# One tiled stage for R, A scores, C v and denominators; G in two stages; normalising among the inverse steps; two batches' u in one tile

## The chip, the cores and the metric

The kernel runs on one core of one Trainium2 chip. The metric is device time in microseconds (us), the median of several executions. A run has a state: fast, or slow when it lies over 1.5% above the fastest run of the same kernel. Engines in the profile: PE is TensorE's matmuls, PEld its weight loads, DVE is VectorE, ACT is ScalarE, POOL is GpSimd, SP is SyncE. L345 is line 345 of the kernel that the profile belongs to, so one statement has different lines in different kernels.

## The reference

Nyström attention with 32 landmarks over 8 batches of 8 heads, then a gated product without a nonlinearity:

```python
q_lm = q.reshape(B, H, m, S // m, D).mean(axis=3)     # B, H, S, D = 8, 8, 576, 64; m = 32
k_lm = k.reshape(B, H, m, S // m, D).mean(axis=3)
A  = softmax(q @ k_lm.T);  Bm = softmax(q_lm @ k_lm.T);  C = softmax(q_lm @ k.T)   # each scaled by 1/8
Z = Bm.T / (norm1(Bm) * norminf(Bm) + 1e-6)
for _ in range(6):
    Z = 2 * Z - Z @ Bm @ Z
x = (A @ Z @ C @ v)              # heads side by side: 4608 x 512
out = ((x @ w1) * (x @ w2)) @ w3 @ w_out
```

The kernel multiplies w3 and w_out together first (the "weight fold") and forms G = Z C v [w1, w2] for each batch. R in the title is the product of Bm with its transpose, from which the inverse steps for Z start. The "up products" are A times G; their elementwise product u is `ab` in the code. The output products are u times (w3 w_out), in chunks of 128 rows.

## The kernel before

The schedule is by hand: the attention of the next batch is a Python generator that yields between stages. The main loop runs one stage after an up product or an output product, so that VectorE's work on a stage hides behind TensorE's work on this batch.

The parts, with cuts marked:

```python
        scores_a(0)                       # A scores, first head group
        yield
        scores_a(1)
        # ... def cv(qd, es, psV): C v of 4 heads and its row sums, then DVE reads psV
        cv(0, es0, small())
        yield
        cv(1, es1, bank())
        yield
        # ...
        def denominators():               # row sums of exp(A scores), into a "big" buffer
            ps = big()
            # ... 8 matmuls into ps[:, 0, 0:QS]
            return ps

        def inverted(i):                  # reciprocals: from PSUM, into PSUM
            sl = slice(QS // 3 * i, QS // 3 * (i + 1))
            nc.vector.reciprocal(out=psS[:, 1, sl], in_=psS[:, 0, sl])

        def mixed():
            rr = psS[:, 1, 0:QS]          # rr is in PSUM
            rhi = pat.tile([128, QS], FP16, name="rhi", bufs=1)
            nc.vector.tensor_copy(out=rhi, in_=rr)
            rmix = pat.tile([128, QS], FP16, name="rmix")
            nc.vector.scalar_tensor_tensor(out=rmix, in0=rhi, scalar=lomask[:, 0:1], in1=rr,
                                           op0=ALU.mult, op1=ALU.add)
            return rmix
        # ... normalise(qd, rmix): 4 matmuls spread rmix over the rows, DVE multiplies
        for it in range(6):               # inverse steps
            # ... 16 small matmuls, then tz_ and sz_ by DVE
            if it == 1:
                psS = denominators()
            elif it in (2, 3, 4):
                inverted(it - 2)
            elif it == 5:
                rmix = mixed()
            yield
        # ... Z, normalise(0), yield, normalise(1), then G in four stages
```

The kernel's PSUM pool has three "big" buffers of 128 x 2 x 512 fp32, one "small" and one "acc" of 128 x 512 each; a "bank" in this text is 512 such columns. The first output chunk uses "acc", the next "big", and so on in turn. Meanwhile POOL adds up the landmarks of a later batch:

```python
    eng.tensor_tensor(out=tr, in0=x[:, :, 0, :], in1=x[:, :, 1, :], op=ALU.add)   # eng = POOL, 128 x 768
    eng.tensor_tensor(out=tr, in0=tr, in1=x[:, :, 2, :], op=ALU.add)              # 128 x 768
```

The softmax here doesn't subtract the row's maximum and nothing guards it: scores larger than these inputs give would overflow.

## Time and profile before

| | before |
|---|---|
| median of 3 runs | 300.87 us (299.02 to 301.57) |
| span of the profiled run | 299.0 us |
| TensorE busy | 276.5 us, 92% |
| mean granted TensorE clock | 0.987 |

The head of the profile's page. The rows below "2" cut the span into 40 slices and give tenths of busy time; PEclk is the granted TensorE clock in tenths.

```profile
PE 276.5 (92%) x4026; PEld 151.7 (51%) x4026; DVE 177.9 (59%) x454; ACT 124.3 (42%) x199; POOL 135.6 (45%) x176
...
PE   6867999999879989999999998999999999999993
...
PEclk9998999999979999999999999999999999999999
```

TensorE is the bound: after the first four slices and up to the last it is at 70% or more in every slice, and at 90% or more in most. So I count a microsecond in which it waits as about a microsecond of time.

What TensorE waited for, in us, times, and the longest (the view of waits, kernel before):

```profile
PE small L183 <- DVE parts L174: 2.7, 2, 2.4
PE big L100 <- DMA qkn<-in_k_dram: 2.7, 1, 2.7
...
PE big L426 <- ACT a_sb L430: 1.9, 9, 0.2
...
PE big L369 <- issue: 1.0, 1, 1.0
```

Most of these belong to start-up and to the passage from the weight fold to the main loop (the 2.4 us). "issue" is a wait for which the trace shows no semaphore.

### The profile page before, as it was taken

The page shows a single profiled execution, that of the slowest core. Times are in us where ns is not written, and L with a number is a line of the kernel's source. Part 1 is how long each engine was busy: PE and PEld are TensorE (multiplying, and loading weights), DVE is VectorE, ACT ScalarE, POOL GpSimd, SP SyncE. Part 2 cuts the span into 40 slices and gives each one's busy share as a digit, 9 for nine tenths or more (in the row PEclk, how much of TensorE's full clock was granted, in tenths as well). Part 3 has the DMA queues.
Part 4 walks back from the last instruction along what each step waited for, and adds up shares of the span by engine and source line. Part 5 has one row for each costly group of instructions (what it writes and reads, how often), then busy time and mean ns, then how long its engine had stood idle before and what let it go on. Part 6 is the DMA issues. An engine that isn't in the chain of part 4 may idle for free.

```text
span 299.0 us, 9452 instructions
## 1 busy us (share of the span) xinstructions
PE 276.5 (92%) x4026; PEld 151.7 (51%) x4026; DVE 177.9 (59%) x454; ACT 124.3 (42%) x199; POOL 135.6 (45%) x176
## 2 busy tenths in 40 slices
PE   6867999999879989999999998999999999999993
PEld 3434555444446447445744663366447535743741
DVE  8922743465476576755765765476666655765720
ACT  2113442233344266236625741474167236525531
POOL 1608132270009958950994499039918940600000
PEclk9998999999979999999999999999999999999999
DMA  6999999939920948975996999379949632013124
GB/s 242 279 268 255 239 232 230 164 38 196 203 54 8 214 110 172 224 165 104 186 219 150 147 201 202 101 140 203 228 111 154 154 107 70 4 30 79 36 58 118
DMA packets 61385, 45.56 MB, mean 152 GB/s; under 512 B 34976, under 2 KB 53408, under 8 KB 61344
## 3 DMA queue, kind: packets, MB, share of 16 engines
q1 hardware_dynamic: 46896, 31.86, 47.1%
q0 software_dynamic: 13632, 11.54, 24.8%
q10 hardware_dynamic: 816, 1.57, 1.4%
q8 instruction: 31, 0.51, 0.7%
q14 instruction: 10, 0.08, 0.1%
HBM read 38.80 MB, written 9.44 MB: 161 GB/s over the span
## 4 chain that ended last, share of the span: by engine, by line
PE 73%; DMA 9%; DVE 9%; ACT 6%; issue 2%; POOL 0%; ACTq 0%; DVEq 0%
PE big L426 16%; PE acc L446 13%; PE big L446 10%; PE acc L490 9%; DMA qkn<-in_q_dram 6%; PE big L412 6%; DVE ab L432 4%; PE big L369 4%; ACT a_sb L430 3%; DMA wof<-in_moe_w_out_dram 2%; PE small L305 2%; PE acc L305 2%; PE big L477 2%; PE big L353 1%; PE big L224 1%
## 5 line engine op out<-in xcount | busy, mean ns | idle before, releaser
L426 PE MATMUL big<-ahat,gt 128*128 128x288 f16 x512 | 75.1, 288 | 3.1 <-ACT a_sb L430 1.9
L432 DVE TENSOR_TENSOR ab<-a_sb,big 128x576 f16<-128x576 f16 x64 | 47.9, 750 | 19.5 <-PE big L426 7.7
L430 ACT CAST a_sb<-big 128x576 f16<-128x576 f32 x64 | 41.0, 640 | 41.6 <-PE big L426 36.1
L426 PEld LDWEIGHTS <-gt 128*128 128x128 f16 x512 | 47.6, 98 | 20.7 <-issue 5.8
L235 POOL TENSOR_TENSOR t<-ect 96x384 f32<-96x384 f32 x16 | 16.0, 997 | 87.0 <-ACT ect L228 86.5
L490 PE MATMUL acc<-wsp,w3t 128*128 128x512 f16 x168 | 42.1, 384 | 1.6 <-DVE wsp L471 0.9
L446 PE MATMUL acc<-w,ab 128*128 128x512 f16 (+1 forms) x192 | 41.0, 382 | 0.1
L446 PEld LDWEIGHTS <-ab 128*128 128x128 f16 (+1 forms) x320 | 23.9, 100 | 32.4 <-issue 9.3
L446 PE MATMUL big<-w,ab 128*128 128x512 f16 x128 | 32.8, 381 | 0.0
L166 POOL TENSOR_TENSOR tr<-qkT 128x768 f32<-128x768 f16 x14 | 23.0, 1643 | 20.7 <-DMA qkT<-qkn 11.0
L418 DVE TENSOR_SCALAR gt<-big 128x1024 f16<-128x1024 f32 x16 | 19.5, 1224 | 17.7 <-PE big L412 17.7
L490 PEld LDWEIGHTS <-w3t 128*128 128x128 f16 x192 | 18.1, 100 | 20.1 <-issue 4.1
L452 ACT ACTIVATE o_sb<-acc 128x512 f32<-128x512 f32 x20 | 11.9, 597 | 37.4 <-PE acc L446 35.5
L167 POOL TENSOR_TENSOR tr<-tr,qkT 128x768 f32<-128x768 f32 x14 | 23.0, 1641 | 1.1
L416 ACT ACTIVATE gt<-big 128x1024 f16<-128x1024 f32 x16 | 16.4, 1024 | 8.6 <-PE big L412 8.6
L412 PE MATMUL big<-wup,zt 64*32 64x512 f16 x512 | 19.0, 380 | 0.8 <-DVE ahat L356 0.8
L483 DVE SCALAR_TENSOR_TENSOR w3t<-big,w3t 128x512 f16<-128x512 f32 x16 | 11.0, 689 | 14.1 <-ACT w3t L482 14.1
L452 ACT ACTIVATE o_sb<-big 128x512 f32<-128x512 f32 x16 | 9.6, 598 | 22.4 <-PE big L446 22.4
L482 ACT ACTIVATE w3t<-big 128x512 f16<-128x512 f32 x16 | 9.5, 597 | 19.9 <-PE big L477 19.5
L228 ACT ACTIVATE ect<-big 96x768 f32<-96x768 f32 x16 | 12.9, 807 | 2.9 <-PE big L224 2.4
L356 DVE TENSOR_TENSOR ahat<-eat,big 128x576 f16<-128x576 f16 x16 | 11.9, 749 | 1.8 <-PE big L353 1.8
L172 POOL TENSOR_TENSOR o<-o,tr 128x256 f32<-128x256 f32 x14 | 11.2, 799 | 1.1
(311 smaller groups left out, 358.9 us busy)
## 6 DMA issues: line engine op xcount, KB each, us to landing
vt<-in_v_dram SPq DMA_DIRECT2D x8, 1152.0 KB, 8.5
qkn<-in_k_dram POOLq DMA_DIRECT2D x8, 576.0 KB, 10.8
qkn<-in_q_dram POOLq DMA_DIRECT2D x8, 576.0 KB, 13.4
out_dram<-o_sb SPq DMA_DIRECT2D x24, 192.0 KB, 2.3
w3f<-in_moe_w_dram SPq DMA_DIRECT2D x6, 512.0 KB, 7.5
out_dram<-o_sb SPq DMA_DIRECT2D x24, 128.0 KB, 2.4
wup<-in_moe_w_dram POOLq DMA_DIRECT2D x4, 512.0 KB, 24.9
wof<-in_moe_w_out_dram ACTq DMA_DIRECT2D x3, 512.0 KB, 7.3
```

The source lines that it names most:

```text
L166: eng.tensor_tensor(out=tr, in0=x[:, :, 0, :], in1=x[:, :, 1, :], op=ALU.add)
L167: eng.tensor_tensor(out=tr, in0=tr, in1=x[:, :, 2, :], op=ALU.add)
L235: nc.gpsimd.tensor_tensor(out=t3[0:NP], in0=e[:, :, 0:3, :], in1=e[:, :, 3:6, :], op=ALU.add)
L412: nc.tensor.matmul(psG[32 * h:32 * h + 32, qd, :], zt[rs, i, h, :], wup[rs, h, w, fs], start=(i == 0), stop=(i == 1), tile_position=(64 * ...
L416: nc.scalar.activation(out=g[:, :, w, fs], in_=psG, func=AXF.Copy, scale=1.0 / ZS)
L418: nc.vector.tensor_scalar(out=g[:, :, w, fs], in0=psG, scalar1=1.0 / ZS, scalar2=None, op0=ALU.mult)
L426: nc.tensor.matmul(p[:, c, 0:HS], st["g"][:, qd, w, 128 * j:128 * j + 128], st["ahat"][qd][:, c, :], start=(qd == 0), stop=(qd == 1))
L430: nc.scalar.copy(out=st["a_sb"], in_=p[:, :, 0:HS])
L432: nc.vector.tensor_tensor(out=st["ab"][:, j, :].rearrange("p (c s) -> p c s", c=2), in0=st["a_sb"], in1=p[:, :, 0:HS], op=ALU.mult)
L446: nc.tensor.matmul(pso[o:o + sz, :], ab[:, j, s0:s0 + sz], w34[:, j, :], start=(j == 0), stop=(j == 7), tile_position=(0, o))
L452: nc.scalar.activation(out=o_sb, in_=pso[:, :], func=AXF.Copy, scale=1.0 / (X64 * X64))
L490: nc.tensor.matmul(psW[j][:, :], turned[j, c // 4][:, a, c % 4, :], wsp[:, b, c, :], start=(c == 0 and a + b == 0), stop=(c == 7 and a == 1))
```

## The change

The intent, as I read it: a change of TensorE's tiling mode costs some 94 ns in the trace of before (a 288-column matmul is followed after 216 instead of 122 ns), so put the small tiled products of a batch into one stage, make G in two stages rather than four, and let u of two batches share one tile, so that no output chunk needs two half-height matmuls. The denominators share a PSUM tile with the C v products. The reciprocals `rr` go to SBUF. And normalising moves up among the inverse steps. The diff, cut to its core:

```diff
-        psR = bank()
+        psX = bank()                        # one tile: R, second C v group, denominators
...
         scores_a(0)
-        yield
         scores_a(1)
...
-        cv(0, es0, small())
-        yield
-        cv(1, es1, bank())
-        yield
+        cv(0, es0, psX if bank is small else small())
+        cv(1, es1, psX[:, 192:] if bank is small else psX)
+        for qd in range(2):
+            for c in range(4):
+                nc.tensor.matmul(psX[32 * c:32 * c + 32, 320:320 + QS],   # denominators
+                                 ...)
+        rr = pat.tile([128, QS], FP32, name="rr", bufs=1)                 # SBUF
         yield
...
-            nc.vector.reciprocal(out=psS[:, 1, sl], in_=psS[:, 0, sl])
+            nc.vector.reciprocal(out=rr[:, sl], in_=psX[:, 320 + sl.start:320 + sl.stop])
...
+        for i in range(3):
+            inverted(i)
+            if i < 2:
+                yield
         for it in range(6):
...
             if it == 1:
-                psS = denominators()
-            elif it in (2, 3, 4):
-                inverted(it - 2)
-            elif it == 5:
                 rmix = mixed()
+            elif it in (2, 3):
+                normalise(it - 2)
             yield
...
-        normalise(0, rmix)
         yield
-        normalise(1, rmix)
...                                          # G: yield after two blocks, not after each
-            steps(at, (0, 0, 0, 1, 1, 1, 2, 2)[j] if b == 0 else 1)
+            steps(at, (0, 0, 0, 1, 1, 1, 1, 0)[j] if b == 0 else (1, 1, 1, 0, 1, 0, 1, 1)[j])
             up(st, j, 1)
+        steps(at, 1)
```

The warm-up matmuls became 20 of 256 columns instead of 10 of 512, to free SBUF for the shared tile.

More of the change, by code (lines that the diff above doesn't have):

```diff
@@ L287, in attention @@
                 sl = slice(32 * h, 32 * h + 32)
-                nc.tensor.matmul(psR[sl, 32 * qd:32 * qd + 32], bt[sl, qd, :], bt[sl, qd, :],
+                nc.tensor.matmul(psX[sl, 128 + 32 * qd:160 + 32 * qd], bt[sl, qd, :], bt[sl, qd, :],
                                  start=True, stop=True, tile_position=(32 * h, 32 * h))
@@ L292, in attention @@
         for qd in range(2):
-            nc.vector.tensor_scalar(out=sz_[:, qd, 0:32], in0=psR[:, 32 * qd:32 * qd + 32],
+            psR = psX[:, 128 + 32 * qd:160 + 32 * qd]
+            nc.vector.tensor_scalar(out=sz_[:, qd, 0:32], in0=psR,
                                     scalar1=nrn[:, qd:qd + 1], scalar2=None, op0=ALU.mult)
             nc.vector.scalar_tensor_tensor(
-                out=tz_[:, qd, :], in0=psR[:, 32 * qd:32 * qd + 32], scalar=nrn[:, qd:qd + 1],
+                out=tz_[:, qd, :], in0=psR, scalar=nrn[:, qd:qd + 1],
                 in1=eye2[:, qd, :], op0=ALU.mult, op1=ALU.add)
         scores_a(0)
-        yield
         scores_a(1)
@@ L315, in cv @@
                                     scalar1=rcr[:, 0:1], scalar2=None, op0=ALU.mult)
-        cv(0, es0, small())
-        yield
-        cv(1, es1, bank())
-        yield
-        ahat = []
-        psS = None
-        def denominators():
-            ps = big()
-            for qd in range(2):
-                for c in range(4):
-                    nc.tensor.matmul(ps[32 * c:32 * c + 32, 0, 0:QS],
-                                     onesq[:, qd].rearrange("p a b h -> p (a b h)"),
-                                     eat[qd][:, QS * c:QS * (c + 1)],
-                                     start=(qd == 0), stop=(qd == 1), tile_position=(0, 32 * c))
-            return ps
+        cv(0, es0, psX if bank is small else small())
[3 more added lines that the diff above has]
+                nc.tensor.matmul(psX[32 * c:32 * c + 32, 320:320 + QS],
+                                 onesq[:, qd].rearrange("p a b h -> p (a b h)"),
+                                 eat[qd][:, QS * c:QS * (c + 1)],
+                                 start=(qd == 0), stop=(qd == 1), tile_position=(0, 32 * c))
+        rr = pat.tile([128, QS], FP32, name="rr", bufs=1)
+        yield
         def inverted(i):
             sl = slice(QS // 3 * i, QS // 3 * (i + 1))
-            nc.vector.reciprocal(out=psS[:, 1, sl], in_=psS[:, 0, sl])
+            nc.vector.reciprocal(out=rr[:, sl], in_=psX[:, 320 + sl.start:320 + sl.stop])
         def mixed():
-            rr = psS[:, 1, 0:QS]
             rhi = pat.tile([128, QS], FP16, name="rhi", bufs=1)
@@ L348, in mixed, with normalise @@
             return rmix
-        def normalise(qd, rmix):
+        ahat = st["ahat"] = []
+        def normalise(qd):
             psD = big()
@@ L396, in attention @@
                                        op0=ALU.mult, op1=ALU.subtract)
-        normalise(0, rmix)
         yield
-        normalise(1, rmix)
-        st["ahat"] = ahat
         g = st["g"] = pat.tile([128, 2, 2, DF], FP16, name="gt")
@@ L419, in attention @@
                                             scalar2=None, op0=ALU.mult)
-                yield
+            yield
     def up(st, j, w):
@@ L432, in up, with down @@
             nc.vector.tensor_tensor(
-                out=st["ab"][:, j, :].rearrange("p (c s) -> p c s", c=2),
+                out=st["ab"][:, j, st["t0"]:st["t0"] + S].rearrange("p (c s) -> p c s", c=2),
                 in0=st["a_sb"], in1=p[:, :, 0:HS], op=ALU.mult)
     rows = out.rearrange("(b p g) f -> b g p f", b=B, g=6)
-    def down(srcs, half, hold, bank):
+    def down(ab, b0, t0, half, hold, bank):
         if half == 0:
@@ L443, in down @@
         for j in range(4 * half, 4 * half + 4):
-            o = 0
-            for _, ab, s0, sz in srcs:
-                nc.tensor.matmul(pso[o:o + sz, :], ab[:, j, s0:s0 + sz], w34[:, j, :],
-                                 start=(j == 0), stop=(j == 7),
-                                 tile_position=(0, o))
-                o += sz
+            nc.tensor.matmul(pso[:, :], ab[:, j, t0:t0 + 128], w34[:, j, :],
+                             start=(j == 0), stop=(j == 7))
         if half == 1:
@@ L454, in down @@
             o = 0
-            for b, _, s0, sz in srcs:
-                while sz:
-                    gi, p0 = divmod(s0, NP)
-                    n = min(sz, NP - p0)
-                    nc.sync.dma_start(out=rows[b, 2 * (gi % 3) + gi // 3, p0:p0 + n, :],
-                                      in_=o_sb[o:o + n, :])
-                    o, s0, sz = o + n, s0 + n, sz - n
+            while o < 128:
+                gi, p0 = divmod((t0 + o) % S, NP)
+                n = min(128 - o, NP - p0)
+                nc.sync.dma_start(out=rows[b0 + (t0 + o) // S, 2 * (gi % 3) + gi // 3, p0:p0 + n, :],
+                                  in_=o_sb[o:o + n, :])
+                o += n
     def fold(pf, wof, w3f, wsp):
@@ L544 @@
         load_w3(1, 1)
-        warm = pf.tile([128, 512], FP16, name="warm", bufs=1)
+        warm = pf.tile([128, 256], FP16, name="warm", bufs=1)
         nc.vector.memset(warm, 0.0)
         psw = big()
-        for _ in range(10):
-            nc.tensor.matmul(psw[:, 0, :], warm[:, 0:128], warm, start=True, stop=True)
+        for _ in range(20):
+            nc.tensor.matmul(psw[:, 0, 0:256], warm[:, 0:128], warm, start=True, stop=True)
         nc.gpsimd.tensor_copy(out=gate, in_=wof[1][:, 0, 0:1])
@@ L589 @@
         load_qk(sts[2], 2)
-    pab = ctx.enter_context(tc.tile_pool(name="pab", bufs=3))
+    pab = ctx.enter_context(tc.tile_pool(name="pab", bufs=2))
     at = attention(sts[1], acc)
@@ L595 @@
         st = sts[b]
-        ab = st["ab"] = pab.tile([128, 8, S], FP16, name="ab")
+        if b % 2 == 0:
+            ab = pab.tile([128, 8, 2 * S], FP16, name="ab")
+        st["ab"], st["t0"] = ab, S * (b % 2)
         if b + 2 < B:
@@ L599 @@
             load_v(sts[b + 2], b + 2)
-        if b % 2 == 0:
-            chunks = [[(b, ab, 128 * t, 128)] for t in range(4)]
-        else:
-            chunks = [[(b - 1, sts[b - 1]["ab"], 512, 64), (b, ab, 0, 64)]]
-            chunks += [[(b, ab, 64 + 128 * t, 128)] for t in range(4)]
+        chunks = range(0, 512, 128) if b % 2 == 0 else range(512, 2 * S, 128)
         for j in range(8):
@@ L620 @@
             bank = (lambda: big()[:, 0, :]) if n // 2 % 2 else acc
-            down(chunks[n // 2], n % 2, hold, bank)
-            steps(at, 2 if n == 6 and nd == 8 else 1)
+            down(ab, b - b % 2, chunks[n // 2], n % 2, hold, bank)
+            steps(at, 2 if b == 0 and n == 0 else 1)
         steps(at, 30)
```

## The prediction

> **What bounds the kernel now.** TensorE. The page has it busy 92% of the span (DVE 59%, ACT 42%, POOL 45%); table of windows: 25.8 of 26.5 us in the batches with four output chunks, about 28 of 29 in those with five. The waits of TensorE sum to only some 17 us, most of it start-up. The first 33 us wait for loads, which the change leaves alone. So what counts is TensorE's time per batch, with its bubbles.
>
> **What it removes.** [...]the last 288-column matmul of an up product is followed after 122 ns by one of its own mode, after 216 ns by a tiled one; for 512 columns 216 and 309 ns. About 94 ns per entry; leaving costs about as much (L310 to L426 103 ns against 12 within the mode). Per batch the instruction order shows 8 to 10 fewer changes of mode. From starts in the timeline, R, A, C v, denominators and the first inverse step took 3.7 us plus six entries, in one stage they need 2.5 plus one, and one 0.42 us inverse step moves to the output phase: 0.8 us saved per batch. G in two stages saves 0.2 to 0.4 us.
>
> **What it adds: waits.** The semaphores of the built program show three new ones on TensorE, in every batch:
> 1. Denominators wait for DVE to have read the second C v group from the same PSUM tile. From the last ones matmul: 0.30 us to the reciprocal, ending with the scaled copy at 0.78. Bubble: about 0.85 us.
> 2. The first output chunk needs the "acc" bank, held until the third reciprocal slice is read. DVE alternates 0.75 us products and 0.46 us reciprocals behind the last up products: ready about 1.5 us after the last up product; the inverse step fills 0.33. Bubble: about 1.1 us.
> 3. Up products now run seven groups back to back. With three big buffers that costs 1.08 us a pair (batch 7, 277.9 to 285.5) against 0.98: 0.3 us with the waits of the A scores. rmix costs 0.2 us before the first normalisation.
>
> Sum: 0.8 to 1.2 us saved against 2.4 lost: odd batches about 1.1 us longer, even ones 1.5. The first batch of the loop has its stage and all three reciprocals directly before the first chunk, and Z, zt and both G stages behind the last: about 2 us longer. Attention inside the weight fold: about even. The whole sits on the critical path. 300.9 + 3 x 1.1 + 3 x 1.5 + 2 is 310.5; I shade it to 309, as the change looks tuned.
>
> **Predicted:** 309.0 us, 301.5 to 314.5 (8 in 10). Faster by over 2%: 0.08; within 2%: 0.24; slower by over 2%: 0.68.
>
> **What would show it.** Right: fewer mode changes; idle before denominators (releaser: DVE scaled copy of C v) of 0.7 to 1.0 us per batch; idle before the first output matmul (releaser: DVE reciprocal) of 0.8 to 1.4 us; time from the second C scores to the first output chunk longer by about a microsecond although its TensorE work is shorter; reciprocals, 0.46 us each, among the last up products on DVE. TensorE's busy share falls.
> Wrong: both bubbles under 0.3 us, and a batch of four chunks taking under 26.5 us.
>
> **What would make it wrong.** DVE running earlier than I chain it (the reciprocals ending before the last up product, say); [...]a larger saving per mode change for fp32 passes than 94 ns; cheaper G stages.

The cost of a mode change is the 94 ns of the trace, and the sum stands at 310.5, shaded to 309. The "fp32 passes" are records of the trace of before: it has 48 records for the 24 fp32 matmuls of one C v group (L305).

## More of the kernel before

The two DVE instructions that make rmix, with minimum, median and maximum duration in ns (the view of one tile, kernel before):

```profile
L344 DVE CAST rhi<-big x8: 297/297/298, 62.0 to 270.0; 128x144 f16<-128x144 f32 x8
L346 DVE SCALAR_TENSOR_TENSOR rmix<-rhi,lomask,big x8: 363/365/365, 62.3 to 270.3; 128x144 f16<-128x144 f16 x8
```

They take the same time in all eight batches. `big` in their names says that their source is a PSUM buffer.

## The result, and the profile after

A ratio here is the mean time of one kernel's fast runs over the mean of the other's fast runs of the same rounds, so it is not quite the ratio of the medians quoted.

| | before | after |
|---|---|---|
| median | 300.5 us (299.02 to 301.57, 4 runs) | 331.87 us (329.29 to 337.81, 4 runs, one of them slow) |
| ratio of fast runs | | 1.1019, 95% interval 1.0897 to 1.1141 |
| span of the profiled run | 299.0 us | 332.1 us |
| TensorE busy | 276.5 us, 92% | 283.0 us, 85% |
| mean granted TensorE clock | 0.987 | 0.954 |

The change made the kernel 10% slower. The direction was foretold. The size was not: 331.87 lies far outside 301.5 to 314.5.

The same head of the page, kernel after:

```profile
PE 283.0 (85%) x4004; PEld 157.0 (47%) x4004; DVE 186.7 (56%) x454; ACT 123.2 (37%) x199; POOL 134.9 (41%) x176
...
PE   6969979998776993899969986999699789979994
...
PEclk9989999999989896999987999899989999999999
```

TensorE now has slices at 60 and 70% all along the run (one at 30%), and the clock has several at 60 to 80%. Idle time grew from 22.5 to 49.1 us (span less busy time), which is 26.6 of the 33.1 us by which the span is longer. The other 6.5 us are longer busy time.

TensorE's waits, kernel after:

```profile
PE big L345 <- DVE rmix L336: 10.5, 5, 2.7
PE acc L435 <- DVE rr L330: 7.5, 7, 1.2
PE acc L321 <- issue: 4.4, 1, 4.4
...
PE acc L321 <- DVE sz__2286 L314: 0.7, 1, 0.7
```

The second line and the last (one such line of 0.6 or 0.7 us for each of the eight batches) are the two foretold bubbles. The first and the third were not foretold, and they are larger.

The two instructions that make rmix, kernel after:

```profile
L334 DVE CAST rhi<-rr x8: 224/988/1672, 55.1 to 299.4; 128x144 f16<-128x144 f32 x8
L336 DVE SCALAR_TENSOR_TENSOR rmix<-rhi,lomask,rr x8: 369/1243/1751, 55.3 to 299.7; 128x144 f16<-128x144 f16 x8
```

These are the same two operations on the same 128x144 elements, with `rr` in SBUF instead of PSUM. Their fastest case is as fast as before or faster (224 against 297 ns), and their slowest is about five times as slow. Something holds them up in some batches only. The timeline of one batch shows what (start, duration, engine, idle time before in brackets; DVE, POOL and PE lines, kernel after):

```profile
168.93 1.04 PE L435 MATMUL acc<-w,ab 128*128 128x512 f16 x4
168.93 1.64 POOL L166 TENSOR_TENSOR tr<-qkT 128x768 f32<-128x768 f16 x1
...
169.51 1.15 DVE L334 CAST rhi<-rr 128x144 f16<-128x144 f32 x1
...
170.65 1.63 POOL L167 TENSOR_TENSOR tr<-tr,qkT 128x768 f32<-128x768 f32 x1
170.70 1.75 DVE L336 SCALAR_TENSOR_TENSOR rmix<-rhi,lomask,rr 128x144 f16<-128x144 f16 x1
...
172.50 0.66 PE L345 MATMUL big<-rmix,selc 128*128 128x144 f16 x4 [2.22 <-DVE rmix L336]
...
172.96 1.91 PE L435 MATMUL big<-w,ab 128*128 128x512 f16 x4
```

The POOL addition at 168.93 ends at 170.57, and rhi ends at 170.66. The next addition ends at 172.28, and rmix ends at 172.45. Each of these two DVE instructions lasts until the POOL instruction that was already running is over, plus about 0.1 to 0.2 us. The last two lines show the sequel: TensorE stood for 2.22 us, and then the same four matmuls of 512 columns that took 1.04 us at 168.93 took 1.91. From start to start they are 427 ns apart, against 216 before the wait: half the clock, and the clock record has 0.5 from 171.93 to 178.76. The batch after the last POOL addition, in the same run, has the same two instructions without that neighbour:

```profile
299.41 0.23 DVE L334 CAST rhi<-rr 128x144 f16<-128x144 f32 x1
299.68 0.37 DVE L336 SCALAR_TENSOR_TENSOR rmix<-rhi,lomask,rr 128x144 f16<-128x144 f16 x1
```

In the kernel before, POOL's same addition also ran next to rhi (213.27 to 214.91), and rhi kept its duration, with its source in PSUM:

```profile
213.27 1.64 POOL L167 TENSOR_TENSOR tr<-tr,qkT 128x768 f32<-128x768 f32 x1
...
214.66 0.30 DVE L344 CAST rhi<-big 128x144 f16<-128x144 f32 x1
```

So beside a POOL addition, and with `rr` in SBUF, the two instructions took 1.15 and 1.75 us here, and 0.23 and 0.37 alone. Through what POOL holds them up the trace does not show. I had not held the new place of `rr` against POOL's additions.

The wait for nothing, kernel after (PE and weight-load lines of the timeline, in the second batch of the loop):

```profile
126.56 0.31 PE L321 MATMUL acc<-eat,onesq 128*32 128x144 f16 x7 [0.67 <-DVE sz__1728 L314]
...
131.24 0.30 PE L321 MATMUL acc<-eat,onesq 128*32 128x144 f16 x1 [4.38 <-issue]
```

TensorE stopped after the seventh of eight equal matmuls into the same tile, for 4.38 us. The transfer records of the queue of kind "instruction" show a packet of 16,384 bytes from 128.53 to 129.75, and TensorE went on 1.49 us after its end.

Where the time went, by stretch. The stretches begin where the landmark products of a batch start (L183), so each holds one batch of the main loop; both spans are cut the same way. Each row is the window in us, its length, the busy times of PE, PEld, DVE, ACT and POOL with their counts, the granted clock, the DMA share and GB/s (view of windows). Kernel before, batches 0, 1 and 6:

```profile
83.66:108.68 25.02, 23.89 (x428) 12.64 (x429) 15.72 (x44) 10.36 (x18) 17.61 (x22) 0.94 0.44 84
108.68:137.45 28.77, 28.26 (x480) 15.48 (x473) 19.12 (x47) 13.81 (x22) 18.06 (x23) 1.00 0.83 169
...
249.82:276.49 26.67, 25.98 (x458) 14.82 (x456) 17.41 (x45) 13.38 (x22) 4.79 (x8) 1.00 0.16 43
```

Kernel after, the same batches. The granted clock is the third number from the end:

```profile
84.19:116.33 32.14, 26.00 (x428) 13.01 (x429) 18.85 (x44) 10.71 (x18) 17.80 (x22) 0.89 0.46 88
116.33:151.89 35.56, 29.09 (x473) 16.37 (x466) 18.90 (x47) 13.23 (x22) 17.76 (x22) 0.90 0.67 126
...
281.08:309.73 28.65, 26.01 (x458) 14.94 (x456) 16.52 (x44) 12.71 (x22) 4.76 (x8) 1.00 0.16 41
```

Batch 6, whose rmix is not held up and whose clock is full, is 1.98 us longer. That is nearest to what the prediction was about, but it holds one thing more, a wait for nothing of 0.48 us. The same kernel with a shifted instruction stream (one of the experiments below) has no such wait in batch 6, where it takes 1.24 us longer than the kernel before:

```profile
279.24:307.15 27.91, 25.72 (x458) 14.81 (x456) 16.52 (x44) 12.70 (x22) 4.78 (x8) 1.00 0.16 43
```

Batches 0 to 5 are 7.1, 6.8, 6.4, 3.1, 5.0 and 2.4 us longer, and the prediction had 2 for the first, 1.1 for the odd and 1.5 for the even ones. Batch 7 is 0.2 us shorter.

### The profile page after: what moved, and what is told of

The parts are those of the page before. It is cut to its first block, busy times and chain, and to the rows that moved or that the text cites. A ratio compares the mean times of both kernels' runs of the same rounds, so it can differ in the third digit from the quotient of the medians.

```text
span 332.1 us, 9399 instructions
## 1 busy us (share of the span) xinstructions
PE 283.0 (85%) x4004; PEld 157.0 (47%) x4004; DVE 186.7 (56%) x454; ACT 123.2 (37%) x199; POOL 134.9 (41%) x176
## 3 DMA queue, kind: packets, MB, share of 16 engines
q10 hardware_dynamic: 816, 1.57, 1.3%
## 4 chain that ended last, share of the span: by engine, by line
PE 66%; DVE 13%; DMA 8%; ACT 8%; issue 3%; POOL 0%; ACTq 0%; DVEq 0%
PE big L417 16%; PE acc L435 11%; PE big L435 10%; PE acc L476 8%; DMA qkn<-in_q_dram 5%; PE big L365 4%; PE big L403 4%; ACT a_sb L421 3%; DVE ab L423 3%; DVE rmix L336 2%; DMA wof<-in_moe_w_out_dram 2%; PE big L345 2%; PE small L305 2%; DVE rhi L334 2%; PE acc L305 2%
## 5 line engine op out<-in xcount | busy, mean ns | idle before, releaser
L417 PE MATMUL big<-ahat,gt 128*128 128x288 f16 x512 | 73.8, 290 | 2.4 <-ACT a_sb L421 1.7
L417 PEld LDWEIGHTS <-gt 128*128 128x128 f16 x512 | 49.1, 99 | 21.9 <-issue 6.8
L421 ACT CAST a_sb<-big 128x576 f16<-128x576 f32 x64 | 40.9, 639 | 49.5 <-PE big L417 44.5
L435 PE MATMUL acc<-w,ab 128*128 128x512 f16 x160 | 43.1, 402 | 7.5 <-DVE rr L330 7.5
L435 PEld LDWEIGHTS <-ab 128*128 128x128 f16 x288 | 26.1, 103 | 39.4 <-issue 16.7
L435 PE MATMUL big<-w,ab 128*128 128x512 f16 x128 | 36.5, 415 | 0.0
L403 PE MATMUL big<-wup,zt 64*32 64x512 f16 x512 | 17.1, 380 | 0.8 <-ACT zt L388 0.5
L345 PE MATMUL big<-rmix,selc 128*128 128x144 f16 x64 | 8.0, 257 | 10.5 <-DVE rmix L336 10.5
## 6 DMA issues: line engine op xcount, KB each, us to landing
qkn<-in_k_dram POOLq DMA_DIRECT2D x8, 576.0 KB, 10.5
```

The source lines that it names most:

```text
L403: nc.tensor.matmul(psG[32 * h:32 * h + 32, qd, :], zt[rs, i, h, :], wup[rs, h, w, fs], start=(i == 0), stop=(i == 1), tile_position=(64 * ...
L417: nc.tensor.matmul(p[:, c, 0:HS], st["g"][:, qd, w, 128 * j:128 * j + 128], st["ahat"][qd][:, c, :], start=(qd == 0), stop=(qd == 1))
L421: nc.scalar.copy(out=st["a_sb"], in_=p[:, :, 0:HS])
L435: nc.tensor.matmul(pso[:, :], ab[:, j, t0:t0 + 128], w34[:, j, :], start=(j == 0), stop=(j == 7))
```

## The experiments

**Theories.** The first, P: the wait for rmix comes from POOL's additions, which hold up rhi and rmix for as long as one of them runs, and only with `rr` in SBUF. Its rivals: DVE is just later in its queue (a matter of order), or SBUF sources are slower as such. The second, B: the two foretold bubbles come from the bank that denominators and reciprocals share with C v and with the first output chunk. The third, F: the wait for nothing is a late packet of instructions, so it belongs to a place in the instruction stream and not to the stage. Its rival: the stage's mode changes or buffers. In four of the recorded expectations the name of a mechanism for P is cut, since no run shows it; where one speaks of "three causes" but lists two, the first is P.

In every experiment the result was correct. The kernel before gave medians of 300.97 to 301.45 us beside them.

### rr back in PSUM

```diff
-        cv(0, es0, psX if bank is small else small())
+        psV0 = psX if bank is small else small()
+        cv(0, es0, psV0)
-        rr = pat.tile([128, QS], FP32, name="rr", bufs=1)
+        rr = psX[:, 320:320 + QS] if bank is small else psV0[:, 128:128 + QS]
```

> The changed kernel with one thing undone: the reciprocals are written to PSUM again (spare columns of the small bank), not to SBUF. Theory[...]: the cast to rhi (0.22 to 1.67 us in the changed kernel) and the rmix operation (0.37 to 1.75 us) wait for the 1.64 us GpSimd additions only because their input lies in SBUF; with PSUM input every one of the eight casts is 0.30 us and every rmix 0.36 us, TensorE's 10.5 us of waiting for rmix falls under 2.5 us, the granted clock rises from 0.954 to at least 0.975, and the time is 308 to 318 us; the two bubbles foretold (0.84 us before the denominators, 1.1 us before the first output chunk) stay. Rival, order: rmix is late because normalising among the inverse steps asks for it too early behind the reciprocals in DVE's queue; then the waits of over 1 us before the normalisation stay, and the time is over 325 us.

Measured: 319.24 us (317.66 to 320.05), ratio 1.0603 (1.0542 to 1.0664). The tile view:

```profile
L335 DVE CAST rhi<-small x8: 296/298/298, 56.1 to 285.3; 128x144 f16<-128x144 f32 x8
L337 DVE SCALAR_TENSOR_TENSOR rmix<-rhi,lomask,small x8: 362/362/366, 56.5 to 285.6; 128x144 f16<-128x144 f16 x8
```

The instruction order is the same; only the place of `rr` differs. The neighbours are there too: in five of the eight batches a POOL addition runs beside rhi and rmix, and they keep their 0.30 and 0.36 us. The durations are back to those of before, the wait for rmix is gone, and the median is 12.6 us lower (12.0 between the means of the fast runs). The wait itself was 10.5 us. A rough count from matmul starts gives 2 to 3 us more: matmuls that start at half rate lose about 9 us in the kernel after, 7 here and 1.5 before; it also takes in some waits for buffers. P stands, and "just later in the queue" falls. Two parts of the expectation were missed: the time lies just above 308 to 318 us, and the granted clock rose to 0.969 and not to 0.975. The wait of the first output chunk stays (7.9 us against 7.5), and so does the stall for nothing (4.6 us):

```profile
PE acc L436 <- DVE small L331: 7.9, 7, 1.6
PE acc L322 <- issue: 4.6, 1, 4.6
```

### The kernel before with only rr in SBUF

```diff
-            nc.vector.reciprocal(out=psS[:, 1, sl], in_=psS[:, 0, sl])
+            nc.vector.reciprocal(out=rr[:, sl], in_=psS[:, 0, sl])
-            rr = psS[:, 1, 0:QS]
+        rr = pat.tile([128, QS], FP32, name="rr", bufs=1)
```

The warm-up tile was halved as in the change, to make room.

> The kernel before with one part of the change alone: the reciprocals go to an SBUF tile (and the warm-up tile is halved as in the change, to make room). Order of work as before. Theory[...]: rhi and rmix, all 0.30 and 0.36 us before, become as long as 1 to 1.75 us where a GpSimd addition runs, although nothing else moved; TensorE needs rmix at once after it, so some batches gain a wait of 1 to 3 us before the normalisation: 301 to 312 us. Rival, order: all durations stay under 0.4 us and the time within 1% of before.

Measured: 305.1 us (303.56 to 307.67), ratio 1.0148 (1.0077 to 1.0219). TensorE waits for rmix 2.5 us in 3 places, and the two instructions are held up again:

```profile
L344 DVE CAST rhi<-rr x8: 224/234/1128, 62.5 to 274.0; 128x144 f16<-128x144 f32 x8
L346 DVE SCALAR_TENSOR_TENSOR rmix<-rhi,lomask,rr x8: 368/738/1755, 62.8 to 274.3; 128x144 f16<-128x144 f16 x8
```

So one moved tile lengthens the old kernel by 1.5% (the smaller warm-up comes with it; the control at the end finds no cost in one). It costs less than in the kernel after (12.6 us): the median of rhi is 234 ns here and 988 there, that of rmix 738 and 1243. The old order makes rmix later in the output products; that it mostly meets the end of a POOL addition there, or one of POOL's shorter instructions, is my reading, and no view here shows it. In these two kernels, with `rr` in SBUF, the two instructions are held up; the new order has them held up more often.

### POOL's additions in four pieces

```diff
-        for h0 in ((0,) if eng is nc.gpsimd else (0, 4)):
-            own, n = ("", H) if eng is nc.gpsimd else ("v", 4)
+        for h0 in ((0, 2, 4, 6) if eng is nc.gpsimd else (0, 4)):
+            own, n = ("", 2) if eng is nc.gpsimd else ("v", 4)
```

`rr` stays in SBUF. Theory P then says: the longest hold is one shorter POOL instruction.

> The changed kernel with the GpSimd landmark additions cut into four pieces each (two heads at a time; 1.64 us becomes about 0.45 us a piece), reciprocals still in SBUF. Theory[...]: the longest rhi falls from 1.67 to under 0.8 us and the longest rmix from 1.75 to under 1.0 us, TensorE's wait for rmix from 10.5 to under 5 us, time 315 to 326 us. Rival, DVE slow for another reason (SBUF source as such, or its queue): durations as in the changed kernel, and no gain.

Measured: 336.2 us (334.39 to 339.1), ratio 1.1181 (1.1085 to 1.1278). An addition now takes 548 ns, and the tile view gives:

```profile
L334 DVE CAST rhi<-rr x8: 224/270/377, 57.1 to 302.0; 128x144 f16<-128x144 f32 x8
L336 DVE SCALAR_TENSOR_TENSOR rmix<-rhi,lomask,rr x8: 368/397/666, 57.3 to 302.3; 128x144 f16<-128x144 f16 x8
```

The slowest case shrank with the POOL instruction, which settles P against "SBUF sources are slow as such". But the time did not fall:

```profile
PE small L183 <- POOL parts L174: 13.0, 4, 4.8
PE acc L435 <- DVE rr L330: 7.2, 7, 1.2
```

Four small POOL instructions take longer than one large one (the additions sum to 61.4 us instead of 45.9), so POOL became the engine that TensorE waits for. The expectation was right about the durations and wrong about the time.

### Denominators and reciprocals in the bank "small"

The edit of the first experiment, and in addition:

```diff
-                nc.tensor.matmul(psX[32 * c:32 * c + 32, 320:320 + QS],
+                nc.tensor.matmul(psV0[32 * c:32 * c + 32, 320:320 + QS],
-            nc.vector.reciprocal(out=rr[:, sl], in_=psX[:, 320 + sl.start:320 + sl.stop])
+            nc.vector.reciprocal(out=rr[:, sl], in_=psV0[:, 320 + sl.start:320 + sl.stop])
```

> The changed kernel with denominators and reciprocals both in the small PSUM bank, which DVE has long finished reading. If my three causes ([...]denominators sharing a bank with a C v group that DVE still reads, first output chunk waiting for the reciprocals to leave acc) are all of the loss: waits before denominators and before the first output chunk under 0.2 us each, no rmix wait over 0.5 us, and 290 to 299 us, faster than the kernel before, because 7 to 10 mode changes of some 94 ns per batch are saved. If the merged stage itself costs (back-to-back up products limited by three big buffers, exposed latencies): 300 to 308 us.

Measured: 309.19 us (306.7 to 310.18), ratio 1.0263 (1.0196 to 1.033), 10 us below the first experiment. Both foretold bubbles are gone from the waits of the loop, but for one wait of 0.5 us of the first output chunk in its first batch. B stands: what the denominators waited for was the shared bank, not the columns they write. (Each of these banks is also one tile of the program; the runs do not tell the two apart.) From the last sums to the first denominator it was up to 0.84 us in the shared bank, and there is no wait once the bank differs, but for the 0.6 us of the attention inside the weight fold, where one bank still serves all.

The expectation named two ranges, 290 to 299 us if these causes were all of the loss and 300 to 308 if the merged stage itself costs. The time lies just above the second, so they are not all. What is left in the waits: 0.5 us in each of six batches, where the inverse step waits for DVE copies that queue behind the reciprocals, and the stall for nothing, in the same stage:

```profile
PE small L322 <- issue: 5.3, 1, 5.3
...
PE big L366 <- DVE sz__1884 L373: 0.5, 1, 0.5
```

### First output chunk in a "big" buffer

The first experiment's kernel, with the order of the two kinds of bank exchanged:

```diff
-            bank = (lambda: big()[:, 0, :]) if n // 2 % 2 else acc
+            bank = acc if n // 2 % 2 else (lambda: big()[:, 0, :])
```

> e1 with one more edit: the first output chunk of a batch takes a big buffer instead of acc, so that it does not wait for the reciprocals. If the acc bank is what the first chunk waits for, its 7.9 us of waiting in e1 vanish; but e5 showed that the next inverse step then waits about 0.6 us for the copies that stand behind the same reciprocals in DVE's queue, so only 0.3 to 0.6 us a batch comes back: 314 to 318 us against 319.2 of e1. If DVE's queue were no limit, the whole 7.9 us would come back: about 311 us.

Measured: 314.77 us (312.21 to 316.87), ratio 1.0439 (1.0359 to 1.0518). The wait of the first output chunk (7.9 us in seven places) is gone and 4.5 us of it are won, since the same wait of about 0.5 us before the next inverse step shows up behind it in six batches. Of this bubble, only the part that the next wait doesn't cover was worth something.

### The instruction stream moved by 120 places

The kernel with denominators in "small", with a warm-up of the same length in smaller pieces. Each matmul is two TensorE instructions (the page of the kernel after counts 4004 matmuls and 4004 weight loads), so 60 more of them move the later stream by 120.

```diff
-        for _ in range(20):
-            nc.tensor.matmul(psw[:, 0, 0:256], warm[:, 0:128], warm, start=True, stop=True)
+        for _ in range(80):
+            nc.tensor.matmul(psw[:, 0, 0:64], warm[:, 0:128], warm[:, 0:64], start=True, stop=True)
```

> e5 with 80 warm-up matmuls of 64 columns instead of 20 of 256 (the same TensorE time while it waits for the first loads), which shifts every later TensorE instruction by 120 places against the 16 KiB packets of the instruction queue. Theory, instruction fetch: in e5 TensorE stands still 5.3 us inside the merged stage of the second batch, waiting for no semaphore, until 1.6 us after such a packet lands; with the packets' borders moved this wait leaves that place, and is under 2 us or elsewhere: 301 to 306 us if it shrinks. Rival, something in the stage itself (a hidden data or bank dependence): the wait stays at the denominators of the second batch at 4 to 5.6 us, time 307 to 310 us.

Measured: 306.3 us (304.38 to 308.82), ratio 1.0167 (1.0087 to 1.0247), against 1.0263 without the shift; the intervals overlap, and the median lies just above the 301 to 306 us expected. What settles it is the trace. The stall of 5.3 us in the second batch is gone; the stage there is unchanged, so it was not the stage. The largest wait for nothing is now 1.4 us, in the next batch. Five of these waits, with the instruction packet beside each, all times in us:

| kernel | packet lands | TensorE goes on | later by |
|---|---|---|---|
| before | 181.49 | 182.81 | 1.32 |
| after | 129.75 | 131.24 | 1.49 |
| denominators in "small" | 124.92 | 126.49 | 1.57 |
| this one | 150.27 | 151.71 | 1.44 |
| spread and shifted (below) | 147.11 | 148.59 | 1.48 |

In the traces of all the runs together TensorE has 34 waits for nothing of over 0.25 us, and each ends 1.22 to 1.59 us after such a packet has landed. F stands.

### The load of v later

Why is that packet late? One guess: the load of v for a later batch (1152 KB) fills the DMA engines at that time, whose share in the trace of the kernel with denominators in "small" is 1.02 to 1.31 from 120 to 128 us. The kernel with denominators in "small", with that load issued after the up products:

```diff
             turn_all(b + 2)
-            load_v(sts[b + 2], b + 2)
...
+        if b + 2 < B:
+            load_v(sts[b + 2], b + 2)
```

> e5 with the load of v for the batch after next (1.15 MB, issued at the start of each batch, in front of the merged stage) issued after the up products instead. Theory: the instruction packet of the second batch comes late because the DMA queues are over 100% busy with this load and the transposes; with the load later, the packet lands sooner and the 5.3 us wait falls under 2 us: 302 to 307 us. Rival (fetch late for another reason): the wait stays over 4 us, 307 to 311 us.

Measured: 310.11 us (308.09 to 313.76), ratio 1.0266 (1.0193 to 1.0338), the same as without the edit. The stall stays at 5.4 us; the profile of this kernel fell on a slow run, so I use it for nothing finer. The load of v is not the cause. Why this one packet comes late stays open; the transposing transfers of the same stretch are a candidate that I did not test.

### A milder form: the merged stage kept, the rest of the steps spread again

The kernel with denominators in "small", with reciprocals among the inverse steps as in the kernel before, rmix in step 4, normalising after Z, and no merging in the attention that runs inside the weight fold (cut to its core):

```diff
-        for i in range(3):
-            inverted(i)
-            if i < 2:
-                yield
...
-            if it == 1:
-                rmix = mixed()
-            elif it in (2, 3):
-                normalise(it - 2)
+            if it in (1, 2, 3):
+                inverted(it - 1)
+            elif it == 4:
+                rmix = mixed()
...
+        normalise(0)
         yield
+        normalise(1)
...
-(1, 1, 1, 0, 1, 0, 1, 1)[j])
+(1, 1, 1, 0, 1, 1, 1, 1)[j])
```

> An attempt to beat both: e5 with the reciprocals and the normalisation put back among and after the inverse steps as before, the inverse steps spread over the last up products, and the first attention (inside the weight fold) not merged. Kept of the change: one tiled stage for R, A scores, both C v groups and denominators, G in two stages, u of two batches in one tile. If back-to-back up products behind three big buffers and the exposed DVE chain are what eats the saved mode changes, each steady batch gets 0.6 to 1.0 us shorter than in the kernel before, and the whole 294 to 299 us, plus up to 6 us if the instruction wait of the second batch stays. Rival, the merged stage itself costs: 303 us or more even without that wait.

Measured: 306.17 us (302.12 to 306.73), ratio 1.0097 (0.9984 to 1.0209). That is above the 294 to 299 us expected, and also above the 305 that the expectation allowed with the stall in. Without the stall (below) it takes 303.65, on the side of the rival, which named 303 or more: the merged stage itself costs something. The waits of about 0.5 us behind the reciprocals are gone, and the fold with the first attention takes 47.5 us again (before 47.8). The stall for nothing is still there, with 5.8 us.

### The changed kernel with only the shifted stream

> The changed kernel with one edit: the warm-up is 80 small matmuls instead of 20 larger ones, which moves every later TensorE instruction by 120 places against the 16 KiB instruction packets. If the 4.4 us wait for nothing in the denominators of the second loop batch is a late instruction packet, it goes or shrinks to under 2 us, and the time falls by 3 to 6 us, to 325 to 329 us; the waits for rmix (about 10.5 us) and for rr (about 7.5 us) stay as they are. If the wait belongs to the stage itself (its mode changes, its buffers), it stays at 4 us or more and the time at 330 to 334 us.

```diff
-        for _ in range(20):
-            nc.tensor.matmul(psw[:, 0, 0:256], warm[:, 0:128], warm, start=True, stop=True)
+        for _ in range(80):
+            nc.tensor.matmul(psw[:, 0, 0:64], warm[:, 0:128], warm[:, 0:64], start=True, stop=True)
```

Measured: 329.71 us (329.32 to 331.3), ratio 1.0953 (1.0894 to 1.1012), against 1.1019 (1.0897 to 1.1141) without it. The stall of 4.4 us is gone, and the longest wait for nothing is 1.3 us; the waits for rmix (10.4 us) and rr (7.5) stayed as expected. The median is 2.2 us lower, a little less than expected, but one of the four runs without the shift was slow: the means of the fast runs differ by 1.0 us. The two intervals overlap, so the time alone would not show it. So the fetch is the smallest of the three causes.

### The milder form with the shifted stream, and with no step among the last up products

First the milder form with the same warm-up edit as just shown, and nothing else:

> e9_spread with the same smaller warm-up matmuls, nothing else. Its 5.8 us wait for nothing in the denominators of the second loop batch should go or shrink to under 2 us; 306.2 us should become 300 to 303 us, within 1.5% of the kernel before. If the wait stays, 305 to 307 us.

Measured: 303.65 us (301.14 to 306.19), ratio 1.0062 (1.0007 to 1.0118). That is just above the range expected. The stall of 5.8 us has become several waits of up to 2.5 us (in a profile of a slow run). Then, on top of it, no step behind the last up product:

> e12_spread_only_shift, and no step of the attention among the last of the eight up products of a batch, so that the last inverse steps come among the output products. If the gaps that remain behind the inverse steps at the end of the up products are bubbles of about 0.5 us a batch, this gains 2 to 4 us more over the kernel without it: 296 to 301 us, level with or up to 1.5% ahead of the kernel before. If the gaps only move to the output products, it is within 1 us of e12_spread_only_shift.

```diff
-(1, 1, 1, 0, 1, 1, 1, 1)[j])
+(1, 1, 1, 0, 1, 1, 1, 0)[j])
```

Measured: 298.46 us (296.48 to 301.56), ratio 0.9901 (0.9848 to 0.9955), within the range expected. It is the fastest kernel, 1% ahead of the kernel before. The busy times from the head of its page:

```profile
PE 274.4 (92%) x4064; PEld 157.6 (53%) x4064; DVE 178.4 (60%) x454; ACT 124.2 (42%) x199; POOL 135.6 (46%) x176
```

Two of its waits:

```profile
PE acc L310 <- issue: 2.2, 2, 1.5
...
PE big L421 <- ACT a_sb L425: 1.7, 8, 0.2
```

Idle time is 22.3 us (296.7 less 274.4), as before (22.5), and busy time is 2.1 us less. That fits the intent, less time in mode changes, once no bubble pays for it; which part of the change gave it was not tested alone. The last step gained 5.2 us of the median (4.8 between the means of the fast runs) over the kernel without it, where 2 to 4 were expected. Up products waited for ACT's buffer (L421 on L425) 4.1 us in the unshifted milder form and 1.7 us here; the rest of the difference I cannot place.

### Control: the kernel before with only the smaller warm-up

> A control for e10_spread_shift: the kernel before with the same smaller warm-up matmuls (80 instead of 10, so its later TensorE instructions move by 70 places against the packets). If the 1% that e10_spread_shift is ahead comes from its stages, this stays within 0.5% of the kernel before (299.5 to 302.5 us), since the kernel before has only one wait for nothing to lose, of 1.0 us. If the 1% comes from the warm-up itself or from its shift alone, this is about 1% faster too, 297 to 299 us.

```diff
-        for _ in range(10):
-            nc.tensor.matmul(psw[:, 0, :], warm[:, 0:128], warm, start=True, stop=True)
+        for _ in range(80):
+            nc.tensor.matmul(psw[:, 0, 0:64], warm[:, 0:128], warm[:, 0:64], start=True, stop=True)
```

(The expectation says 70 places; as each is two instructions it is 140.) Measured: 300.66 us (299.97 to 302.53), ratio 0.9997 (0.9966 to 1.0027). So the 1% of the fastest kernel is not the warm-up or the shift alone.

## Why the prediction was right or wrong

**Right: what bounds the kernel, and the direction.** TensorE's busy share fell from 92 to 85%. The direction is not luck: with `rr` back in PSUM, so with the foretold bubbles but without the step that failed, the kernel is still 6% slower than before (the fetch stall, which was not foretold, is in that too).

**Right: the two bubbles.** The denominators start 0.78 to 0.84 us after the last sums (foretold 0.85), and the first output chunk 1.13 us late (foretold 1.1). Taking both away gave 10 us.

**Right: fewer changes of mode.** By the shapes of the matmuls, batches 1 to 6 had 30 or 34 changes of mode each and have 23 or 24 (foretold: 8 to 10 fewer).

**Right: G.** Its busy time fell from 19.0 to 17.1 us over eight batches, 0.24 us each (foretold 0.2 to 0.4).

**Right, as far as one batch shows: the sum for a batch without other trouble.** Batch 6 became 1.98 us longer where about 1.5 was foretold, but 0.48 us of waiting for an instruction packet are in that. In the shifted kernel, without this wait, it is 1.24 us longer. The up products are as foretold too: in batch 6, 59 intervals between matmuls of up products lose 0.39 us to waits, against 0.06 in 55 before, so 0.32 us more where I put 0.3. (The sum in the prediction has a slip: its terms make 310.7 and not 310.5.)

**Wrong: "Attention inside the weight fold: about even."** That stretch went from 47.83 to 49.46 us. With one bank for everything it has three waits of 0.5 to 0.7 us, and without the merging (the milder form) it takes 47.5 again.

**The step that failed: "rmix costs 0.2 us before the first normalisation."** It cost 10.5 us in five waits, up to 2.7 each, and 12.6 us of the median with the half-rate matmuls that follow. I costed rmix with the durations of the kernel before (0.30 and 0.37 us), although the change gives it another source. Here a duration read from one trace did not hold once the operand's memory and POOL's instructions beside it were others. This step does not make up the whole miss: with it undone the kernel takes 319.24 us, still above 314.5. The rest is what follows here and the 1.6 us of the weight fold; how it divides was not measured.

**Missed: the fetch of instructions.** The trace of before had a wait for nothing of 1.0 us, which I took as noise. In the kernel after one of 4.4 us fell in the second batch. By the ratios of the three pairs of kernels with and without the shift it is worth some 1 to 3 us (1.1019 and 1.0953, 1.0263 and 1.0167, 1.0097 and 1.0062); in each pair the intervals overlap, so the size is uncertain.

**Missed: the clock.** In the kernel after, each of the four longest waits for rmix (1.9 to 2.7 us) has a stretch of 3.41 or 6.83 us at half clock that begins between 0.6 us before its end and 1.2 us after it, so these waits cost more than their length; the fifth, of 1.4 us, has none. In the main loop the stretches begin whole multiples of 3.41 us apart (96.84, 107.08, 127.56, 171.93, 206.07 and 240.20 us), and the delay varies: the wait of 2.22 us that ended at 172.50 was followed by half rate at once, the one of 2.73 us that ended at 106.13 by full rate (216 ns at 106.39) until 107.08, and one of 2.41 us that ended at 84.19 by no stretch at half clock before 96.84. Of this the prediction has nothing. By my rough count of starts it is about 8 us of the kernel after (9 to 10 less 1.5 to 2), part of which belongs to each of the causes above.

## What to carry to other kernels

When a change moves an operand between PSUM and SBUF, cost each instruction that reads it anew, and look at which POOL instructions run beside it: here a VectorE instruction of 0.37 us lasted up to 1.75, as long as POOL's longest beside it. Before merging stages, list for each PSUM bank who must be done with it before the next writer: the two waits on shared banks were 0.84 and 1.1 us a batch here. And a wait that the trace puts down to no semaphore may move with the instruction count alone (5.3 us here were gone after 120 more instructions), so test a gain of 1% or less with a kernel that shifts the stream and changes nothing else.
